# Linformer attention and an MLP mixer on one core: scores as four 64x64 matmuls, keys turned in pairs, a new order of the work

## The chip, the core and the metric

The kernel runs on one core of a Trainium2 chip. The core has a matrix engine (TensorE, called PE in the profile; its weight loads are listed apart as PEld), a vector engine (VectorE, DVE), a scalar engine (ScalarE, ACT), a general engine (GpSimd, POOL) that here issues most loads and stores, and SyncE (SP), which issues transposing transfers. Each engine works through its own list of instructions in order; semaphores make one engine wait for another. Matmuls write to PSUM, a memory of 128 partitions and 8 banks of 512 float32 columns; everything else is in SBUF, also of 128 partitions. A matmul holds a stationary operand ("weights", at most 128x128) in the array and streams a moving operand of up to 512 columns through it. If the stationary operand uses only 64 rows (partitions of its inputs) or only 64 columns (partitions of its output), the array can be used in halves or quarters.

The metric is the device time of one execution in microseconds, the median over runs.

## The reference

For each of 8 batches and 8 heads (sequence 1024, head dimension 64) the reference computes attention with keys and values projected to 64 positions, and sends the result through a mixer MLP. Cut to what matters:

```python
k_proj = einsum('ks,bhsd->bhkd', E, k)            # [8, 8, 64, 64]
v_proj = einsum('ks,bhsd->bhkd', F, v)
scores = scale * matmul(q, k_proj.transpose(0, 1, 3, 2))   # [8, 8, 1024, 64]
attn = softmax(scores)
x = matmul(attn, v_proj)      # heads side by side: [8, 1024, 512]
h = relu(x^T @ w_tok1) @ w_tok2           # 1024 -> 256 -> 1024, mixes tokens
u = x + h^T
out = u + relu(u @ w_ch1) @ w_ch2         # 512 -> 1536 -> 512, mixes channels
```

Inputs and output are float32; the kernel computes in bfloat16 with float32 sums.

## The kernel before

The work of a batch has two parts. The **front** is attention and token mixing up to u; the **back** is channel mixing, done in halves of a batch (512 rows each), sixteen in all. Both mixings use a seven-product scheme for 2x2 blocks (S_t, wT1, wT2, wS hold sums of blocks), so that the back is 84 matmuls of 256 columns "up" (L1193) and 84 "down" (L1301) per half batch, 2688 of the kernel's 3845. The front of batch b + 1 is woven into the back of batch b; batch 0's front has nothing to hide behind.

Steps of a front, with the lines that the profile shows:

- `load_heads` (the transfer is recorded at L362): keys, values and queries come in as bfloat16, two heads a transfer (256 KB in SBUF) for batch 0, four heads after that. Row `p` of the sequence block is stored with its 8 neighbours, so that a head's queries lie as [128 partitions, 8, 64].
- `kv_proj` (L529): the projections. For each of 8 steps there is one matmul with `E` (output partitions 0 to 63) and one with `F` (partitions 64 to 127), 64 stationary columns each; batches 2 to 7 use 512 moving columns, batch 1 two calls of 256, batch 0 four groups of two heads with 128. Copies (recorded at L340 on ScalarE, L338 on VectorE) take keys to `kp` or `kb`, and values to `vb`, each of them twice: `vb` of a head is a block-diagonal 128x130 operand whose 65th columns are ones.
- Keys are turned, so that the head dimension lies on partitions: for batches 0 and 1 by `k_transpose` on TensorE (L570, one 64-row matmul a head against an identity), for later ones by a transposing transfer (`k_transpose_dma`) from `kb`. The result `kT` of a head is block-diagonal too, 128x128: sequence rows of even and odd number lie on partitions 0 to 63 and 64 to 127 of `qT`, and each half meets its own copy of the keys while the other two quarters of the array hold zeros.
- Queries are turned by TensorE (`q_transpose_pe`, L618, batch 0 and 1) or by a transposing transfer.
- `scores` (L634): one matmul of 512 columns a head into one bank; ScalarE takes its exponential to `a_t` (L643).
- `attend` (L657) and, from batch 3 on, `attend_whole` (L693): per head, four matmuls of 130 columns with `a_t` as stationary operand and `vb` as moving; VectorE takes the reciprocals of the sums and multiplies into `x_sb`.
- Token mixing: by parts of 128 channels in batch 0 (`token1_part` L1073, `token2_part` L1105, `u_transpose_pe` L1134), whole in batch 1 (L724, L748), by seven products in the others (L888, L1004).

Nothing in this order is decided on the chip. Every step is a job of a `Planner`; the string `ORDER` gives the place of each job in one list for all engines (and so each engine's own list, the queues of GpSimd and SyncE among them), and `SPOTS` the PSUM bank of each use. `FILLS` names the places where a matmul on zeros (`blank`, L440) is put in front of a TensorE job. Both strings are the result of a search made beforehand with estimated durations (the second and third arguments of `pl.add`), and are read back in `plan`. Loads of batch 0 are issued first, by GpSimd: keys, values and queries by pairs of heads, then the token weights `wt1`, `wt2`, then the channel weights.

Of the kernel before, what the change touches and what calls it, by code (L numbers as in the profile page):

```python
# [15 lines left out]
    "0P0Q0R0S000T0201030U0W0X040V0s0+1G0-050u0t1I1H0x1J0y0z1L1O101209241N0v1K1P0w131M26111A1B1Q1D0625071S"  # L16
    "1T172A1g18080A1C0B1E0C1a1415191b2C1R1k2B1h1i1o1c1F1l1j1d1n1m161X1p1Y1q2D1s1U1r2E1Z1t0D1u1e1f1x1V1W1v"
    "0E272H2F0G0H1w29281+2V2I211y1-2a0F1z222b20232G2P2W2Q2M2c2J2f2X2S2g2N2K2Y2Z2d2L2R2h2e2T2O2k2i2l2U2t0I"
    "2m2p2n332u2j2x2q2r2o342-2y0J0K2v3B2s300Y2z35313C0Z2w2+320c3T3P0a3R3l3Q3F3U3D3V3J3K360d370e3W3X3Z3m38"
    "0L0N413G3p3Y3a3q3n3b3o0b3S0g0O3c420M0h3r3L3s3E3d390f3M0i3f433e3A3t3g3H0j3u3I4547465044513v48493w5x4g"  # L20
    "4h523x5y5z4k4i4A4j3y534B4J604D4l3N4o4E5-544K5+4m0o614C4F3h4p554r4L3z4n4s0p574R4q0k584u5A4S0q3-4H0l4t"
    "3j0m62634v563O654O646N666P4w594P6O5C404T6Q3+4x6e6W4Q6f6X6g3i674U6T6B6Y6Z696L5I684I3k6U6V4V6R6J6K6a6A"
    "5J6S6b6F6G5D4G6c6d0r5K5M6C4MAH6D6E6j4y4W6H5BAI6r6I0n5N6s6k6l4N4Y6u6t6m6n6h6i6o6v4Z5L5P705O6p4X6w714c"
    "726x5Q6q736z5R4a5a6y6+6-75745S5E7677787B5bAJ7C797H5T7A5c7I4d5U7D7K7E5i7J7LAK6M7NA97M7Q7FAB7G7O7R7S7P"
    "AL4b7T5V5G4z5F4+AAAOAC5W5Y5X7V5j4eAN7UAM7XAQ7W4-5f7Z7YAP7a7c7g5g7e7d7h5h7f5d7i5lAV5kAh5mAW7jAZAb5e5H"
    "Ai7bAX5n5ZAcAaAe7l7pAfAYAd5p7qAmAj817r7sAg7nAnAkAlAuAT7tAxAo5qAvAw7o7u7m82ApAr7wAy85Az5r5o7vAqAsAtA+"
    "B583B0A-5t7x86BB887y847-BC7z7k89B1B6ASB2B7BDAUARB3B880BE8J87B9BF7+8BBAB4BJ8ABM8KBGBK8LBLBHBI8M8NBP8D"
    "BNBS8OBQBO5uBR8Q8b8P8CBTBVBU8EBXBW8RBYBZ8T8y8S8cBaBb8UBc90Bd8+Be918V94Bf5v8zBgAD8WBj92Bh95Bk9E97Bi9F"
    "93Bn968FBo8-Bl9GBr9I98Bs9A9J9HAFBmBp8HBq8I99AEEn8dBuBw8X9CEp9B9L9M8jBxBvBt9WBy9OErEoEq8Z9PAG9X8g8k8h"
    "BzB+5sEj8YEk4f9DB-9aC48iC19Y8mC08lC29bC59dC79Z9c8G9e8nC68e9K8aC89f8oCB8f9g9NEs9iC99QCC8pCDEl8q8uCA9j"  # L30
    "CG9hCH8r8sC3CJE-8vEzCEF09R9oEx8wCFCLE+CNEyCO9p9kCbEv5wF1F4CK9qCP9wEmF5CQF29SF39mCMCR9xCcCIF69U9TCSCf"
    "F7CUCVCgF8Cd9y9tFBCXFCCT8t9uF9FDCYCWEw9VFGCeCtFH9vFACu9lCZCiCaFOCjDWFPCvCw9zChFECxFIDXCyFFFL9+ClCkCz"
    "FJFMDYFN9-FQ9nFRC+FSCmFKCnCoC-A1FTD0FUFVD9DaA2D1DbFWEuDAD3CpA3FXFYDeFZFaEtDfDZDcDdFd9rD4D5CqDh9sIrDB"
    "DiFeA0FbFfItFcCrA5DkFh8xInFgIsIvD2FiCsIoFjA6DoFnIuFoFkA7D7FlFmDHFrD8DpDlDgFpFvDIFsDjFqFtDmDsA4DnFwDt"
    "DJFyDEFxF+D6DFFzDqG0F-DvDGDCG8G1DrDwFuDKG2G3DyG9G5G4DLG6GBE4DMDuGCDzE5DDDxE8DNIpIqIwE9GAGDGFD+GGGEGH"
    "EBDOECE6GIDPGKD-G7J3EAGJGLEDDSJ4E7I-DQIzJ0J1EEEGGRJ2EFJ5J8GSGNDTGPGMEMJ9J6J7JDEHDUDRE0JAJBJEE1EIENGT"
    "GfEOE2GgGVJCEKA8EUGjGWEVJFGOGkJGERJHEWGQELGhESJNGmGiGUETJOGYGXJIGnI+JKDVGZGpGxJLIxGbEXEJGqJMJPHaGyJJ"
    "GaHcEYMrJSJTGcJQGzGdJRJUE3EZHeG-EbGlJVGeIyJWHbG+H0EPJXH2GoGrHdJYJZGsHfHgHiJaJbHjH3JcEQJdEcEaHhJfHsJh"
    "EdJgJiH5MsHlGtJeEfHmJjHoEgH1H6HtJkJmEhHpJlJnH4EiHkGuJoHnJrHDJsGvJpJqH7JvHqH8JtJwH9HAHBJzJxJuJ+HrMvK0"
    "HwK2HxMxK1JyHEK3K4HzJ-K5MtK6HFHuHIKCK9MyHLK7H+MwHvKDMzI0I1HMKFHyKAHCK8EeHNKGI8HGI9GwHJICHKKJIAKHKEHO"  # L40
    "IBIDKKKIKMHPKLH-HQM+KNHHIFKON7IGI2KBHSN8IEKPN3IIHTNCHRKRN4MuKVIJIHI3HUKTIKN5KWNDIQKZN9ILN1M-KaN6KXHW"
    "IRNAKYNBISIMNEKjNHHXNIKUI4NFNGI6IYHYNJKkIZNKNLNRKcKdI7NOKnIOKoKlKfIVNSNPNQNMIWKmIaKQNNKSHVKgKbI5NTIX"
    "NUKeINLeKqK-L0IbNVKhN2IcNYL3KiITNZNWKrNaL4NbIPL6NXIdNcL7IUNdKpIeIfNeKsNfIgL1KtIjKvNgNlN0NhIhNjKwL2L5"
    "L8IkLHL9LBNmKxNiNkKuKzLfNnIlLCQwNoLiLINqNpNrNsLALDIiKyQzLjLkLgLJK+LELFNtNuNvLlNwLmHZNxLwLGLMLxQ-NzNy"
    "N+O1O2LnN-LNLOL+R1LyO4LpLPO6O5O0O8LhR0O9L-LzQ+LQLoM1LSO7LqO3LRLrLTQvImOBOGOALuODOCOELvQyLsMCM2OHQxOJ"
    "M4LtOKM0LKONLLM3M5OIMDR2LUMGOLOOMHM6OPLWMEMJMFOQOSOMM7LVOFLXMKOTMIOVMLOXORLYOZLaR7MOMMRBLbMPMQMUM8R9"
    "R8MNRCOaRDLcREOWMVRARFOdOnMWOoMSMAObMcMBR4RIOrMZRJOeOcOsOpRKOuRNROOYOqR5RPMdLZOvOgOxRGOyRVRHOUMaP3Oh"
    "RWM9MeRLOfOjRSMbR6OiRTMTMfRMOkP4RaRbOlRUMRMgOmP7RQOtRXRRMhRYP5RZMjMXPiOwRcMYPmP6RdReOzMiRfPjO+PkMkMn"
    "P8RgPLR3RhMlPnPARiPlMoRjPBP9PqPoRkUzPpPDMpRlRnPCO-PMRoRpV1PFRmRqPEPrMmMqPtRrV3PNRsRtPuPsPGPHLdP0V5Ru"
    "RvPTPwRzP1V2PIV4RwPJRxRyP+P2R+PUPxPvS1PVS5R-S2PQS0S3S6U+P-PyPzQGS8SAQ0SKQ2QHQ1S9SBQIPKS4Q3QJSCPRS7SL"  # L50
    "SDQ4Q5SFQKSNPSSESHQ6QLSGQ8PWSPPXQNQ7SISOPYSRV0V6U-QASSSMQBQ9QOSTSQPOQCPaSUPPSWSXQMVBPbSVQQVCV7QRV9QY"
    "SJQDSdQPPZPcV8SZVAQZVDVEVFSbQSQTSeSfPeVIShSYSgPfQaSiQgVJVGVKQUSkQWPgQEVNScQhSrVOVPVHPdQdVLVVQeSsSlSv"
    "VWVSSwVMSaQiQfSnStSjSoVQTnVTTmVUSyVXT7VRSuSzToQjSmSxVaVYQXVZQVVcVdVeS-S+QFSpSqVbQkVfQbT0TqT8T1QlQcQn"
    "TBT2T9VgVhQmViTrTCTsVjTEQoTpVkVlQpTAVnQrVpTFTHQsTDTtVqVmTIU2QtVoTuTGT3VrVsVtTwVuTvTJU3TxVvVzVwT5TKU6"
    "TyVxVyU4T+V-TzTPV+U7T6W0U0TLT-U5W1W5U9W6UKT4TNW2UAW3ULU1W7WATQW8QqUCTRW4TMW9TOUOUDUPTUWCU8UMTVWDPhQu"
    "WBTXWEWKWFWHTWUBWGTYTaWITZUNURUETbUSUFTSUQWLWNTcWPTTUTTeWOTdUWWRTiUXWJUUWdTfWZWaWSWMUVTjWeWrWfTgWbWT"
    "WUWgWQUcWsWhWiWcUdWvWkUGTkWVUYUeWtWuWlUkX7UaUIUHUlUhWjWWUmWnUiThUJWXUjX8WwWmXBWyX9UZWoWzUnXAWYWpWqUo"
    "UbW-XCX0UpUfWxW+XEXDXFXGUgUrXHXJXqUqUsXmX1XoXKY6XnUvUtXIX2XPXrY7XuX3UuYAUwXsX5XLX4XNUxX6XpXvXQY8YBYD"
    "XwXxXtXRYEXXXUXyY9XzYGYOXYY0XVTlYHY1XWXMYPYSYQYCXaY2YTYFYRYVXZXbYWY3XcXOYUYXYIXSXeYaXfYJYKYbYgY4XTYM"
    "YYXgYZYcXdYhYeX+YLYiXiYNX-UyXhYlXjYmYdYfYoXkYxYnYjYkYsYpYqYrXlYuYvY5Z5YtYyYwZ7YzY-Y+Z0Z1Z6Z2Z8Z3Z9Z4"  # L60
    "ZA"
)
SPOTS = (
    "3142613427007634307612314207426673103142670116377263077463615421302542313140341042376756766765577757"
    "5677567656575676776765677012402414535120342241300556757665577667657656757670616706243123414252534103"
    "1030217767656565656566664736746140534132101500435323042776765656566656666572764742531530452410441031"
    "0201575666656765656667373675631354342042453105031532566576565656665666657476371031410300534153443125"
    "327676656565666566662726706421140051545432102101214756"
)
FILLS = (9, 9, 14, 14, 14, 14, 14, 14, 16, 16, 16, 16, 16, 16, 27, 27, 27, 42, 42, 72, 81, 81, 84)  # L70
# [118 lines left out]
def kernel(  # L189
# [86 lines left out]
    vb = tile_of([P, H, 2, D1], BF16, "vb")  # L276
    kT = tile_of([P, H, 2, KP], BF16, "kT")
# [3 lines left out]
    kp = wS[:KP, 0:2].rearrange("p n a b -> p (n a b)").rearrange("p (h r d) -> p h r d", h=H, r=2)  # L281
    kb = tile_of([P, H, 2, D], BF16, "kb")
# [9 lines left out]
    a_t = [tile_of([P, 2, S2], BF16, f"a{i}") for i in range(2)]  # L292
# [4 lines left out]
    rdn_t = [tile_of([P, 2, 4], F32, f"rdn{i}") for i in range(2)]  # L297
# [9 lines left out]
    nc.vector.memset(kT, 0.0)  # L307
    nc.vector.memset(kb, 0.0)
# [34 lines left out]
    def scalar():  # L343
        return None, "A"
# [162 lines left out]
    def kv_proj(b, h0, hn, due, block=False, apart=False):  # L507
# [3 lines left out]
        t = 8 * max(cols, 128) / 2400 + 0.22  # L511
        if block:
            k_to = [kb[i * KP : (i + 1) * KP, hs, i, :] for i in range(2)]
        else:
            k_to = [kp[:, hs, i, :] for i in range(2)]
        v_to = [vb[i * KP : (i + 1) * KP, hs, i, 0:D] for i in range(2)]
        of = {"k": (0, k_to, "kb" if block else "kp", ET_sb, k_sb), "v": (KP, v_to, "vb", FT_sb, v_sb)}

        def side(names):
            bk = Bank(stream[0], full=False)  # L520
# [5 lines left out]
            def mm():  # L526
                for si in range(NSI):
                    for n in names:
                        nc.tensor.matmul(  # L529
                            view(n), of[n][3][:, si, :], of[n][4][:, hs, si, :],  # L530
                            start=(si == 0), stop=(si == NSI - 1),
                        )

            pl.add(
                "PE", t, t, mm, reads=[("EFT", 0), ("EFT", 1)] + [(n, h) for n in names for h in heads],
                takes=[bk], prio=due,
                after=[("vb", i, h) for i in range(2) for h in heads] if "v" in names else (),
            ).mms = NSI * len(names)
            unit = scalar() if block else next(sides)
            for n in names:  # L540
# [1032 lines left out]
```

## Time and profile before

Three runs gave 416.75, 417.02 and 419.17 us; the median is 417.02.

| | |
|---|---|
| profiled execution: span from first to last instruction | 415.5 us (no other time of it is given) |
| TensorE clock granted | 1.000 |
| TensorE busy | 409.8 us, 3845 matmuls |
| VectorE busy | 358.8 us |
| ScalarE busy | 227.4 us |
| GpSimd busy | 66.7 us |
| matmuls of the back (L1193, L1301), busy | 198.8 and 181.8 us |
| scores (L634), 64 of them, busy | 22.8 us |
| exponentials (L643), 64 of them | 37.4 us, 600 ns each |
| first matmul on an input (L529) | at 8.57 us |
| first matmul of the back (L1193) | at 31.95 us |
| last 6 matmuls start | at 411.44 us |

A row of the timeline gives the start, the length, the engine, the line, the operation with the tiles it writes and reads, and how many equal ones in a row were merged. In the page's groups, "x64 | 22.8, 379 | 0.1" reads: 64 of them, 22.8 us busy in all, 379 ns a piece, 0.1 us of idle time of the engine in front of them. Matmuls overlap in the array: the length of one includes its way through, so the time that a stream of them costs is read from one start to the next. In brackets stands how long the engine sat idle before the row, and what released it.

### The profile page before, as it was taken

How to read it: one execution, taken by the hardware profiler on the slowest of the kernel's cores; microseconds unless marked ns; L12 is line 12 of the kernel's file. 1: busy time of each engine (PE TensorE's matmuls, PEld its weight loads, DVE VectorE, ACT ScalarE, POOL GpSimd, SP SyncE). 2: the span in 40 equal slices, each digit the busy share in tenths (PEclk: the TensorE clock that was granted, in tenths of full speed). 3: DMA queues.
4: the chain of work that ended last, by engine and by line, in shares of the span. 5: the costliest groups of instructions: out<-in, count | busy, mean ns of one | idle time of the engine just before them, and what ended most of it. 6: DMA issues, size and time to landing. Idle time of an engine off the chain costs nothing.

```text
span 415.5 us, 9448 instructions
## 1 busy us (share of the span) xinstructions
PE 409.8 (99%) x3845; PEld 349.0 (84%) x3845; DVE 358.8 (86%) x774; ACT 227.4 (55%) x434; POOL 66.7 (16%) x105
## 2 busy tenths in 40 slices
PE   8999999999999999999999999999999999999996
PEld 4589888688898889888898888988898889998885
DVE  2489898899899988989988997888999998897696
ACT  1758875376745655564465537365573656254620
POOL 8444111013010400130101220102200010000100
PEclk9999999999999999999999999999999999999999
DMA  8999999996999898679979899488982403212314
GB/s 162 204 202 205 206 206 224 168 138 101 232 167 209 137 233 134 104 170 221 217 106 189 113 184 198 83 165 135 231 152 53 100 11 144 50 53 52 153 50 154
DMA packets 96827, 62.47 MB, mean 150 GB/s; under 512 B 62096, under 2 KB 92304, under 8 KB 96784
## 3 DMA queue, kind: packets, MB, share of 16 engines
q0 software_dynamic: 35088, 45.09, 55.4%
q1 hardware_dynamic: 61056, 16.00, 22.8%
q10 hardware_dynamic: 640, 0.79, 0.5%
q8 instruction: 30, 0.49, 0.5%
q14 instruction: 13, 0.11, 0.1%
HBM read 59.24 MB, written 16.78 MB: 183 GB/s over the span
## 4 chain that ended last, share of the span: by engine, by line
PE 94%; DMA 2%; POOL 2%; DVE 1%; issue 0%; POOLq 0%; DVEq 0%
PE psum L1193 35%; PE psum L1301 35%; PE psum L1004 4%; PE psum L888 4%; PE psum L529 3%; PE psum L634 3%; DMA v_sb<-in_v_dram 2%; PE psum L693 2%; PE psum L657 1%; PE psum L1105 1%; PE psum L748 1%; PE psum L1073 1%; PE psum L724 1%; DVE x_sb L674 1%; POOL k_sb L362 1%; PE psum L618 0%
## 5 line engine op out<-in xcount | busy, mean ns | idle before, releaser
L1301 PEld LDWEIGHTS <-G 128*128 128x128 bf16 x1344 | 130.2, 98 | 17.2 <-issue 0.2
L1301 PE MATMUL psum<-wc_sb,G 128*128 128x256 bf16 x768 | 104.0, 273 | 0.0
L1193 PEld LDWEIGHTS <-wc_sb 128*128 128x128 bf16 x768 | 73.9, 98 | 10.1 <-issue 0.6
L1215 ACT ACTIVATE G<-psum 128x512 bf16<-128x512 f32 x96 | 57.3, 601 | 40.7 <-PE psum L1193 40.2
L1301 PE MATMUL psum<-wT,G 128*128 128x256 bf16 x576 | 77.8, 273 | 0.0
L1229 DVE TENSOR_TENSOR G<-G 128x512 bf16<-128x512 bf16 (+1 forms) x140 | 69.1, 514 | 0.5
L1193 PEld LDWEIGHTS <-wT 128*128 128x128 bf16 x576 | 55.6, 98 | 7.5 <-issue 0.4
L1193 PE MATMUL psum<-uT,wc_sb 128*128 128x256 bf16 x384 | 56.8, 273 | 0.0
L1193 PE MATMUL psum<-S,wT 128*128 128x256 bf16 x384 | 56.8, 273 | 0.0
L1193 PE MATMUL psum<-S,wc_sb 128*128 128x256 bf16 x384 | 56.5, 273 | 0.0
L643 ACT ACTIVATE a<-psum 128x512 bf16<-128x512 f32 x64 | 37.4, 600 | 26.3 <-PE psum L634 25.9
L1341 DVE TENSOR_TENSOR o<-psum,u 128x512 f32<-128x512 f32 x59 | 40.3, 684 | 4.7 <-PE psum L1301 3.2
L1335 POOL DMA_DIRECT2D out_dram<-o x30 | 16.3, 546 | 159.4 <-DVE o L1341 124.6
L1221 ACT COPY ub<-psum 128x512 f32<-128x512 f32 x48 | 28.1, 589 | 21.9 <-PE psum L1193 18.1
L1174 DVE CUSTOM_DVE_ANT_0 G<-psum,ub 128x512 bf16<-128x512 f32 x48 | 32.8, 683 | 6.9 <-PE psum L1193 6.5
L1236 ACT COPY psum<-psum 128x512 f32<-128x512 f32 x48 | 27.7, 577 | 19.3 <-PE psum L1193 7.7
L1174 DVE CUSTOM_DVE_ANT_0 G<-psum,ua 128x512 bf16<-128x512 f32 x48 | 32.8, 684 | 5.8 <-PE psum L1193 3.0
L1221 ACT COPY ua<-psum 128x512 f32<-128x512 f32 x48 | 28.1, 591 | 17.2 <-PE psum L1193 17.0
L362 POOL DMA_DIRECT2D v_sb<-in_v_dram x18 | 13.4, 745 | 132.7 <-DMA uT<-u 76.7
L1193 PE MATMUL psum<-uT,wT 128*128 128x256 bf16 x192 | 28.7, 273 | 0.0
L710 DVE TENSOR_TENSOR x_sb<-psum,rdn 128x512 bf16<-128x512 f32 x40 | 27.5, 688 | 0.9
L634 PE MATMUL psum<-qT,kT 128*128 128x512 bf16 x64 | 22.8, 379 | 0.1
(109 smaller groups left out, 548.2 us busy)
## 6 DMA issues: line engine op xcount, KB each, us to landing
out_dram<-o POOLq DMA_DIRECT2D x30, 512.0 KB, 4.8
k_sb<-in_k_dram POOLq DMA_DIRECT2D x14, 512.0 KB, 9.3
v_sb<-in_v_dram POOLq DMA_DIRECT2D x14, 512.0 KB, 6.5
q_sb<-in_q_dram POOLq DMA_DIRECT2D x14, 512.0 KB, 12.3
wc_sb<-in_moe_w_ch_dram POOLq DMA_DIRECT2D x6, 256.0 KB, 11.6
wc_sb<-in_moe_w_ch_dram POOLq DMA_DIRECT2D x4, 384.0 KB, 15.1
k_sb<-in_k_dram POOLq DMA_DIRECT2D x4, 256.0 KB, 7.4
q_sb<-in_q_dram POOLq DMA_DIRECT2D x4, 256.0 KB, 8.9
```

What stands on the lines that cost most here:

```text
L362: return lambda: nc.gpsimd.dma_start(out=dst, in_=src)
L634: lambda: nc.tensor.matmul(bank(bk), kT[:, h].rearrange("p c k -> p (c k)"), qT[:, h].rearrange("p j s -> p (j s)"), start=True, stop=True,),
L643: lambda: nc.scalar.activation(out=a_t[h // 2 % 2][:, h % 2], in_=bank(bk), func=ACT.Exp, scale=scale),
L710: lambda: nc.vector.tensor_tensor(out=x_sb[:, :, h * D : (h + 1) * D].rearrange("p (n c) d -> p n c d", n=2), in0=view()[:, :, :, 0:D], in ...
L1174: nc.vector._custom_dve(TENSOR_ADD_SAT, out=out, in0=in0, in1=in1, s0=FMAX, s1=0.0)
L1193: nc.tensor.matmul(t[:, c, :], w1_of(n, dd, 2 * m + c), a_of(j, n, dd), start=(n in (1, 7) and c == 0 and dd == 0), stop=(c == 1 and dd == 1),
L1215: lambda: nc.scalar.activation(out=G[:, n, cs], in_=view(src), func=ACT.Relu),
L1221: 512, lambda: nc.scalar.copy(out=dst, in_=view("y")), writes=[(name, s % 2)],
L1229: 512 * len(both), lambda: f(out=G[:, n, c], in0=G[:, a, c], in1=G[:, b, c]), ps=False,
L1236: 512, lambda: nc.scalar.copy(out=view("y"), in_=view("x")), takes=[bk["y"]],
L1301: nc.tensor.matmul(to, G[:, G_OF[n], cc, t * P : (t + 1) * P], w2_of(n, cc), start=(n in opens and (t == 0 or alone) and cc == 0), stop=(c ...
L1341: 512, lambda: nc.vector.tensor_add(out=dst, in0=view(src), in1=u_of(sh, dh)),
```

## The change

- **Scores.** `scores` now takes pairs of heads. Per pair `g` there are two banks, one for each half (even and odd sequence rows). Four matmuls with 64 rows and 64 columns of the array each: half `half` of the partitions (`rows`) holds the turned keys of head `2g + i` and its queries; the output goes to partitions `64 i` and up of bank `(g, half)`. The order within a pair alternates the quarters. A call does one pair in batch 0 and two pairs (four banks) in the other batches, so there are two calls a batch instead of eight.
- **Layouts that follow.** `a_t` holds a pair of heads on its partitions, with the halves side by side (four tiles instead of two). `vb` is block-diagonal over the two heads of a pair (half as large), `kT` holds 64 columns a head, the same on both partition halves, without zeros. `attend` works on a pair and a half of the sequence; the number of its matmuls (32 of 130 columns a batch), reciprocals and multiplies is as before. Values are copied once instead of twice; keys are copied to both places of `kb`, now for all batches (`kp` is gone). `kT` and `kb` are no longer cleared at the start.
- **Keys of batches 0 and 1.** `k_transpose` turns a pair of heads with one full 128x128 matmul against the identity, and its result is taken out with one copy instead of two. The transposing transfer of the later batches has half the size.
- **Order.** `ORDER`, `SPOTS` and `FILLS` are new throughout. There are 21 filler matmuls instead of 23. Loads of batch 0 are issued in the order v0, k2, q0, k0, q2, v2, k6, q6, k4, v4, q4, wt1, wt1, v6, wt2 (the number is the first of the two heads); before it was k0, q0, v0, k2, v2, q2, k6, k4, v4, q4, q6, v6, wt1, wt1, wt2. Job estimates change slightly (the projection's 0.22 us of extra time is now 0.03, and jobs carry a `mode`).

```diff
-FILLS = (9, 9, 14, 14, 14, 14, 14, 14, 16, 16, 16, 16, 16, 16, 27, 27, 27, 42, 42, 72, 81, 81, 84)
+FILLS = (20, 20, 20, 20, 20, 20, 20, 20, 20, 20, 20, 20, 20, 20, 20, 20, 33, 33, 49, 67, 92)
...
-    vb = tile_of([P, H, 2, D1], BF16, "vb")
-    kT = tile_of([P, H, 2, KP], BF16, "kT")
+    vb = tile_of([P, HP, 2, D1], BF16, "vb")
+    kT = tile_of([P, H, KP], BF16, "kT")
...
-    kb = tile_of([P, H, 2, D], BF16, "kb")
+    kb = tile_of([P, HP, 2, D], BF16, "kb")
...
-    nc.vector.memset(kT, 0.0)
-    nc.vector.memset(kb, 0.0)
...
             for n in names:
-                for i in ((0, 1) if n == "k" else (1, 0)):
-                    copy(
-                        unit, cols, of[n][1][i], lambda n=n: view(n),
-                        writes=[(of[n][2], i, h) for h in heads], uses=[bk],
-                    )
+                for i in range(2):
+                    rows = slice(i * KP, (i + 1) * KP)
+                    if n == "v":
+                        copy(
+                            unit, cols // 2, vb[rows, pairs, i, 0:D], lambda i=i: odd("v", i),
+                            writes=[("vb", h) for h in heads if h % 2 == i], uses=[bk],
+                        )
+                    else:
+                        copy(
+                            unit, cols, kb[rows, pairs],
+                            lambda i=i: odd("k", i)[:, :, None, :].to_broadcast([KP, hn // 2, 2, D]),
+                            writes=[("kb", h) for h in heads if h % 2 == i], uses=[bk],
+                        )
...
         def mm():
-            for h in range(hn):
+            for h in range(0, hn, 2):
                 nc.tensor.matmul(
-                    view()[:, h, :], kp[:, h0 + h].rearrange("k r d -> k (r d)"),
-                    ident[:KP, :KP], start=True, stop=True,
+                    view()[:, h : h + 2, :].rearrange("p h k -> p (h k)"),
+                    kb[:, (h0 + h) // 2].rearrange("k r d -> k (r d)"), ident, start=True, stop=True,
                 )
...
-    def scores(h, due):
-        bk = Bank(stream[0], full=False)
-        pe(
-            1, 512,
-            lambda: nc.tensor.matmul(
-                bank(bk), kT[:, h].rearrange("p c k -> p (c k)"),
-                qT[:, h].rearrange("p j s -> p (j s)"), start=True, stop=True,
-            ),
...
+    def scores(pairs, due):
+        bks = {(g, half): Bank(stream[0]) for g in pairs for half in range(2)}
+        def mm():
+            for g in pairs:
+                for half, i in ((0, 0), (1, 1), (0, 1), (1, 0)):
+                    rows, to = (slice(n * D, (n + 1) * D) for n in (half, i))
+                    nc.tensor.matmul(
+                        bank(bks[g, half])[to], kT[rows, 2 * g + i],
+                        qT[rows, 2 * g + i].rearrange("p j s -> p (j s)"), start=True, stop=True,
+                    )
...
+        for (g, half), bk in bks.items():
+            act(
+                512,
+                lambda g=g, half=half, bk=bk: nc.scalar.activation(
+                    out=a_t[g][:, half], in_=bank(bk), func=ACT.Exp, scale=scale
+                ),
+                writes=[("a", g, half)], uses=[bk],
+            )
...
+    def attend(g, half, due, span):
+        def unit(jn, due):
...
+            def mm():
+                for k, jj in enumerate(jn):
+                    for c in range(2):
+                        at = (2 * half + jj) * P
+                        nc.tensor.matmul(
+                            view()[:, k, c].rearrange("p i d -> p (i d)"), a_t[g][:, c, at : at + P],
+                            vb[:, g].rearrange("k i d -> k (i d)"), start=True, stop=True,
+                        )
...
+        if span == 2:
+            unit((0, 1), due)
+        else:
+            unit((0,), due)
+            unit((1,), due)
...
-        unit(0.4, lambda t: scores(0, t))
-        unit(0.4, lambda t: scores(1, t))
-        for h in range(H):
-            if h + 2 < H:
-                unit(0.4, lambda t, h=h: scores(h + 2, t))
-            if b >= WHOLE:
-                unit(0.5, lambda t, h=h: attend_whole(h, t))
-                continue
+        unit(1.0, lambda t: scores((0, 1), t))
+        for g in range(HP):
+            if g == 1:
+                unit(1.0, lambda t: scores((2, 3), t))
             for half in range(2):
-                unit(0.25, lambda t, h=h, half=half: attend(h, half, t))
+                unit(0.5, lambda t, g=g, half=half: attend(g, half, t, 2 if b >= WHOLE else 1))
```

More of the change, by code (lines that the diff above doesn't have):

```diff
@@ L21 @@
[L21 to L30, printed above, removed]
@@ L510, in kv_proj @@
         cols = hn * D
[L511 to L517, printed above, removed]
+        t = 8 * max(cols, 128) / 2400 + 0.03
+        pairs = slice(h0 // 2, (h0 + hn) // 2)
+        of = {"k": (0, ET_sb, k_sb), "v": (KP, FT_sb, v_sb)}
         def side(names):
-            bk = Bank(stream[0], full=False)
+            bk = Bank(stream[0], full=hn == H)
             def view(n):
@@ new lines, in scores @@
+    def scores(pairs, due):
[8 more added lines that the diff above has]
+                    )
+        heads = [2 * g + i for g in pairs for i in range(2)]
+        j = pl.add(
+            "PE", len(pairs) * MM[512], len(pairs) * MM[512], mm,
+            reads=[(n, h) for n in ("kT", "qT") for h in heads], takes=list(bks.values()), prio=due,
+            after=[("a", g, half) for g in pairs for half in range(2)],
+        )
+        j.mms, j.mode = 4 * len(pairs), 3
+        for (g, half), bk in bks.items():
[5 more added lines that the diff above has]
+                writes=[("a", g, half)], uses=[bk],
+            )
@@ L844, in one @@
             )
[L846 to L847 removed]
+        one(5, wS[:, 0], a21, a22, add=True)
         one(7, wS[:, 2], a11, a21)
[L850 removed]
+        one(6, wS[:, 1], wS[:, 0], a11, deps=(5,))
         one(3, a21, a12, wS[:, 1], deps=(6, 7, 5), after=wt1_all)
@@ L1424 @@
         q_transpose_pe(hp, due + 1.5)
-        for h in (2 * hp, 2 * hp + 1):
-            scores(h, due + 2)
-        for h in (2 * hp, 2 * hp + 1):
-            for half in range(2):
-                attend(h, half, due + 3)
+        scores((hp,), due + 2)
+        for half in range(2):
+            attend(hp, half, due + 3, 1)
     for p0, pn in PARTS:
```

233 lines of the change are left out of this document (96 added, 137 removed).

## The prediction

> **What bounds the kernel now.** I read the page from the top: busy shares, the slices, the chain, then the group of the scores.
>
> ```profile
> span 415.5 us, 9448 instructions
> ...
> PE 409.8 (99%) x3845; PEld 349.0 (84%) x3845; DVE 358.8 (86%) x774; ACT 227.4 (55%) x434; POOL 66.7 (16%) x105
> ...
> PE   8999999999999999999999999999999999999996
> ...
> PE 94%; DMA 2%; POOL 2%; DVE 1%; issue 0%; POOLq 0%; DVEq 0%
> ...
> L634 PE MATMUL psum<-qT,kT 128*128 128x512 bf16 x64 | 22.8, 379 | 0.1
> ```
>
> TensorE (PE) is the bound in every slice but the first and last. The 379 ns of one score is a pipelined length and not what it costs. The cost is the step from one start to the next, which the timeline of PE gives:
>
> ```profile
> 92.55 0.38 PE L634 MATMUL psum<-qT,kT 128*128 128x512 bf16 x1
> 92.76 0.60 PE L1193 MATMUL psum<-S,wc_sb 128*128 128x256 bf16 x4
> ```
>
> A score costs 0.216 us (0.21 in these rounded rows, 0.216 over all its steps); likewise a 256-column matmul costs 0.109, a 130-column one 0.057. From 24.03 to its last matmul near 412.1 PE never waits: of its gaps beyond those steps all but two of 0.1 us lie at changes of the tile shape. A projection shows such a change:
>
> ```profile
> 149.97 0.82 PE L1301 MATMUL psum<-wT,G 128*128 128x256 bf16 x6
> 150.71 0.40 PE L529 MATMUL psum<-k_sb,EFT_sb 128*64 128x512 bf16 x1
> 150.72 0.40 PE L529 MATMUL psum<-v_sb,EFT_sb 128*64 128x512 bf16 x1
> 150.95 0.38 PE L529 MATMUL psum<-k_sb,EFT_sb 128*64 128x512 bf16 x1
> 150.96 0.38 PE L529 MATMUL psum<-v_sb,EFT_sb 128*64 128x512 bf16 x1
> ...
> 152.25 0.38 PE L529 MATMUL psum<-k_sb,EFT_sb 128*64 128x512 bf16 x1
> 152.25 0.38 PE L529 MATMUL psum<-v_sb,EFT_sb 128*64 128x512 bf16 x1
> 152.56 0.61 PE L888 MATMUL psum<-u,wS 128*128 128x256 bf16 x4
> ```
>
> Two things are to be seen. Keys and values, in two halves of the array's columns, start within 0.01 us and step together by 0.215: two matmuls for the price of one. And a visit to another shape costs extra: the last L1301 starts at 149.97 + 5 x 0.109 = 150.52, the next start comes 0.09 late, the second pair 0.02 late, the first L888 0.31 after the last pair instead of 0.215, the one after it 0.01 late. Together **0.22 us a visit**, 0.11 a change.
>
> The first 24 us are bound by loads, which land one after another; the GpSimd timeline shows the pace:
>
> ```profile
> 12.72 0.56 POOL L362 DMA_DIRECT2D wt_sb<-in_moe_w_tok_dram  x1 [0.56 <-DMA v_sb<-in_v_dram]
> 13.99 0.54 POOL L362 DMA_DIRECT2D wt_sb<-in_moe_w_tok_dram  x1 [0.72 <-DMA q_sb<-in_q_dram]
> ```
>
> One load of 256 KB in 1.27 us. Values that are third, fifth and ninth in line start their projections at 9.22, 12.47 and 17.59: place p lands at 12.4 + 1.27 (p - 5).
>
> **The change, part by part (after 24 us).**
> - Scores, batches 1 to 7: 56 matmuls x 0.216 = 12.10 become 28 groups of four 64x64 matmuls. If the four run at once, a group costs one step, 28 x 0.216 = 6.05: **-6.05**. The rows show the two column halves at once, but never two row halves. So a group lies between 0.216 (all at once) and 0.432 (row halves in turn); below 0.216 is excluded, since 512 columns pass. I take 0.216: nearest is the projection's row, and each row half here has its own bank and its own input rows.
> - Changes of shape: 10 visits (8 projections, 2 turnings of keys in batch 1) become 22 (8 projections, 14 scoring calls), one scoring call standing directly before a projection and sharing a change. 22 x 0.22 - 0.11 - 10 x 0.22 = **+2.53**. Entry to a four-tile shape is not in the trace; I take the projection's price, bounds 0 and 0.4 a visit.
> - Keys of batch 1 turned pair by pair: 8 x 0.04 = 0.3 become 4 x 0.056 = 0.22: **-0.08**.
> - Attention times values stays at 32 matmuls of 130 a batch, with as many reciprocals and multiplies: 0. The exponentials stay 64 x 0.600. ScalarE's copies of values halve in width (0.590 to about 0.372, the row of 256), two clears on VectorE and half of the keys' transposing DMA go: 0, for PE waits for none of these after 24 us.
> - Four banks are now taken at once, and each first attend needs two exponentials: about 0.2 after the group, 2 x 0.60, 0.1 to start, so 1.5 us. The new order leaves 1.5 to 2.0 us of PE work there in batches 1, 2, 3, 4 and 7 and over 3.9 in 5 and 6. ScalarE's order is fixed by the plan too; one more copy of 0.6 in between shows as a PE wait. I take **+0.2**, bounds 0 and 7 x 0.6 = 4.
>
> Sum after 24 us: -6.05 + 2.53 - 0.08 + 0.2 = -3.4.
>
> **The start.** Batch 0 also needs less PE work: scores 0.86 less, two filler matmuls 0.43, two changes 0.22, key turns 0.08, 1.6 in all. It buys nothing: PE waits for loads there. What counts is when PE stops waiting and what is left then. The new queue order is values 0, keys 2, queries 0, keys 0 (4th, 11.2 us), and so on; queries 4 are 11th (20.1), the last values 14th (23.9 where they landed at 21.4), second token weights unchanged (26.4). After queries 4: transposes 0.45, ScalarE copies of 0.2 each and the 1.01 one to about 22.0, scores, then three exponentials to 23.9, attends and a token matmul group to 24.8, where the last values' projection stands. Before had 388.1 us from 24.03 on. At 24.8 the new order has 24 token matmuls less ahead (1.34) and one projection more (0.67): 388.1 - 3.6 - 0.67 = 383.8, plus the 0.2 above and 0.3 for the last pair's reciprocals and multiplies (4 x 0.17 + 4 x 0.416 = 2.3 us of VectorE, covered by about 2 us of PE work). PE ends at 24.8 + 384.3 = 409.1, against 412.1: **-3.0**. Bounds on the start: 0.8 better (no wait for the exponentials) to 1.5 worse (one load slot late).
>
> The end keeps its 3.4 us of last adds and stores. Span 412.5. The profiled execution's time is given by its span alone; the median of the runs, 417.02, lies 1.5 above it, and I add that: **414.0 us**, 0.7% less.
>
> **The Trainium skill** on the four tiles: its page TensorE: Matmul & The Clock Gate (Part 3, What overlaps and what doesn't) has weight loads overlap running matmuls only where the row group differs. By that the second column half of each row half would load only after the first had run, and each group would be two rounds with bare loads. The trace disagrees for the two column halves: pairs on the same 128 rows step at 0.215. No run here shows two row halves.
>
> **Rivals.**
> 1. Row halves take turns. For: no row shows two row halves running together. Against: the column halves do. A group then costs 0.432, so nothing is saved but 2.53 of changes is paid: 414.0 + 6.05 + about 0.4 in batch 0 = **420.5**, slower than before. It decides from about 0.32 a group, where 28 x 0.108 eats the gain of 3.0.
> 2. Two rounds with bare weight loads, 2 x (0.216 + 0.110, the length of a 64-column load): 28 x 0.436 = 12.2 more, **426**. Against: the step of 0.215 above. The rule just cited says this.
> 3. The new order waits where the old did not: exponentials late by a copy in most batches, or a key, query or value load late (the whole order is new, and nothing in it gives way on the chip). For: the 1.5 to 2.0 us above are tight. Against: old waits after 24 us are 0.2 in all. Price 2 to 4: **416 to 418**.
> 4. The start does better: PE's savings there count because the last values no longer gate. 1.5 less: **412.5** or below.
>
> **How the numbers follow.** Forecast 0.60 (412 to 415.5), rival 1 0.09, 2 0.03, 3 0.13, 4 0.15. 1% is 4.2 us, about what a measurement of this kernel can tell: faster means below 412.85. Rival 4 and a quarter of the forecast's spread lie there: 0.30. Rival 2 and half of rival 1 lie above 421.2: 0.08. The rest, 0.62, is within 1%. The range leaves out rivals 1 and 2 and the tails of 3 and 4: 411.5 to 418.5.
>
> **What would show it.** Four L636 matmuls starting within some 0.02 us and the next four 0.216 later (right), or two starting 0.2 after the other two (rival 1). The last matmul before a scoring call and the first after it show the visit's 0.22. PE idle, released by ScalarE's exponentials, would be rival 3; the last values' projection at 24 or at 25 decides the start. I am wrong above all if a group's step is not one matmul's, or if the first 27 us lose more than a load slot.

## The result

The changed kernel took **418.75 us** (median of 19, 416.86 to 423.01) where the kernel before took 417.18 (19, 416.59 to 419.17) beside it: a ratio of 1.0049 (here and below of the means), interval [1.0029, 1.0069]. Forecast were 414.0, in a range that ended at 418.5. Two later measurements of the same two kernels, on two different chips, gave 0.9997 [0.9981, 1.0013] and 1.0002 [0.9984, 1.0019]. So the change brought nothing in any of the three, and in one it cost half a per cent. Both facts have to be explained.

The page of the changed kernel, in the order used for before: span, engines, TensorE by slices, the chain.

```profile
span 418.4 us, 9560 instructions
...
PE 407.5 (97%) x3899; PEld 344.6 (82%) x3899; DVE 357.4 (85%) x771; ACT 221.3 (53%) x429; POOL 66.8 (16%) x105
...
PE   8799999989999999999999999999999999999995
...
PE 83%; DVE 7%; DMA 5%; POOL 2%; issue 1%; ACT 0%; SPq 0%; POOLq 0%; DVEq 0%
```

TensorE was at 9 in every slice of before but the ends; now the ninth slice (83.7 to 94.1 us) has an 8, and its share of the chain is 83% in place of 94%. (The second slice, 10.5 to 20.9 us, has a 7: batch 0 has less work for TensorE now, and waits for loads and copies there.) Its group of scores has 128 rows of 64x64 and names the wait:

```profile
L636 PE MATMUL psum<-qT,kT 64*64 64x512 bf16 x128 | 10.4, 389 | 2.6 <-DMA kT<-kb 1.8 <-ACT kT L335 0.6 <-ACT qT L335 0.2
```

The timeline of TensorE (start, length, line, times in a row) shows an ordinary scoring call, and then the one that waited:

```profile
63.91 0.38 PE L1287 MATMUL psum<-wc_sb,G 128*128 128x256 bf16 x2
64.22 0.63 PE L636 MATMUL psum<-qT,kT 64*64 64x512 bf16 x8
64.78 0.61 PE L1179 MATMUL psum<-S,wc_sb 128*128 128x256 bf16 x4
...
90.80 0.60 PE L1179 MATMUL psum<-S,wc_sb 128*128 128x256 bf16 x4
93.21 0.63 PE L636 MATMUL psum<-qT,kT 64*64 64x512 bf16 x8 [1.82 <-DMA kT<-kb]
93.77 0.61 PE L1179 MATMUL psum<-uT,wT 128*128 128x256 bf16 x4
94.22 0.77 PE L1179 MATMUL psum<-uT,wc_sb 128*128 128x256 bf16 x4
94.78 1.06 PE L1179 MATMUL psum<-S,wT 128*128 128x256 bf16 x4
95.64 1.06 PE L1179 MATMUL psum<-S,wc_sb 128*128 128x256 bf16 x4
```

Eight scores and both changes of shape lie between 64.02 (the last L1287 start, 63.91 + 0.109) and 64.78: 0.760 us, of which 0.109 belong to the L1287. The first group of four and the second stand 0.240 us apart in the unrounded rows. At 91 us the same call begins 1.89 us late because the turned keys of batch 2 have not landed. A little later four matmuls take 0.86 us (94.78 to 95.64) in place of 0.44. The windows (of their columns: the stretch, its length, PE busy, and after POOL the granted clock, DMA share and GB/s) say why:

```profile
91.00:95.00 4.00, 2.18 (x22) 1.25 (x20) 2.03 (x4) 1.92 (x4) 0.00 (x0) 0.94 1.39 130
95.00:100.00 5.00, 5.00 (x38) 3.95 (x36) 3.36 (x11) 3.51 (x7) 0.74 (x1) 0.71 0.61 138
```

The granted clock is at half for 3.41 us, from 94.51. Before had 1.00 in both of these stretches. TensorE's gaps beyond a normal step in that stretch add up to 1.64 us.

What the late keys have beside them shows in the lists of SyncE and GpSimd. Before, the keys of batch 2 were turned ahead of the first half of u (the second goes out at 91.26):

```profile
78.59 1.23 SPq L553 DMA_TRANSPOSE kT<-kb  x1
80.69 13.63 SPq L796 DMA_TRANSPOSE uT<-u  x2
```

Now they come behind it, and so does a load of values that the landing of this half of u releases:

```profile
79.36 2.82 SPq L783 DMA_TRANSPOSE uT<-u  x1
82.41 1.73 SPq L599 DMA_TRANSPOSE qT<-q_sb  x1
84.24 1.83 SPq L557 DMA_TRANSPOSE kT<-kb  x1
...
84.32 0.74 POOL L357 DMA_DIRECT2D v_sb<-in_v_dram  x1 [9.73 <-DMA uT<-u]
```

The end is the third difference. The last rows of TensorE and of ScalarE's queue, after:

```profile
409.31 0.60 PE L1179 MATMUL psum<-S,wc_sb 128*128 128x256 bf16 x4
409.74 1.47 PE L1287 MATMUL psum<-wT,G 128*128 128x256 bf16 x12
411.05 2.79 PE L1287 MATMUL psum<-wc_sb,G 128*128 128x256 bf16 x24
...
413.68 1.65 ACTq L1321 DMA_DIRECT2D out_dram<-o  x3
```

and the same queue before:

```profile
411.06 1.43 ACTq L1335 DMA_DIRECT2D out_dram<-o  x3
```

Before, the first of these three stores was issued 0.93 us ahead of the last matmul's start (411.99). Now it is issued 0.11 behind it (413.57). The one of 256 KB among them went out 0.93 ahead before and 0.51 behind now. From the last matmul's start to the end of the span it is 3.46 us before and 4.80 after: to the last issue 0.76 and 1.41, from there to its landing 1.77 and 2.45.

### The profile page after: what moved, and what is told of

Same layout as the page of the kernel before. It is cut to its first block, busy times and chain, and to the rows that moved or that the text cites. A ratio compares the mean times of both kernels' runs of the same rounds, so it can differ in the third digit from the quotient of the medians.

```text
span 418.4 us, 9560 instructions
## 1 busy us (share of the span) xinstructions
PE 407.5 (97%) x3899; PEld 344.6 (82%) x3899; DVE 357.4 (85%) x771; ACT 221.3 (53%) x429; POOL 66.8 (16%) x105
## 4 chain that ended last, share of the span: by engine, by line
PE 83%; DVE 7%; DMA 5%; POOL 2%; issue 1%; ACT 0%; SPq 0%; POOLq 0%; DVEq 0%
PE psum L1179 32%; PE psum L1287 31%; PE psum L990 4%; PE psum L874 4%; PE psum L671 3%; PE psum L520 3%; DMA q_sb<-in_q_dram 3%; DMA kT<-kb 2%; PE psum L636 2%; DVE x_sb L691 1%; DVE G L1215 1%; PE psum L1091 1%; PE psum L711 1%; POOL k_sb L357 1%; PE psum L735 1%
## 5 line engine op out<-in xcount | busy, mean ns | idle before, releaser
L1287 PEld LDWEIGHTS <-G 128*128 128x128 bf16 x1344 | 129.8, 98 | 17.3 <-issue 1.4
L1287 PE MATMUL psum<-wc_sb,G 128*128 128x256 bf16 x768 | 100.5, 273 | 0.0
L1201 ACT ACTIVATE G<-psum 128x512 bf16<-128x512 f32 x96 | 56.1, 601 | 42.3 <-PE psum L1179 41.7
L1287 PE MATMUL psum<-wT,G 128*128 128x256 bf16 x576 | 75.7, 273 | 0.0
L691 DVE TENSOR_TENSOR x_sb<-psum,rdn 128x256 bf16<-128x256 f32 (+1 forms) x88 | 46.3, 540 | 1.9
L651 ACT ACTIVATE a<-psum 128x512 bf16<-128x512 f32 x64 | 34.6, 603 | 10.1 <-PE psum L636 10.1
L671 PE MATMUL psum<-vb,a 128*128 128x130 bf16 x256 | 25.0, 222 | 0.3 <-DVE vb L333 0.2
```

The costliest lines, as they stand in the source:

```text
L651: lambda g=g, half=half, bk=bk: nc.scalar.activation(out=a_t[g][:, half], in_=bank(bk), func=ACT.Exp, scale=scale),
L671: nc.tensor.matmul(view()[:, k, c].rearrange("p i d -> p (i d)"), a_t[g][:, c, at : at + P], vb[:, g].rearrange("k i d -> k (i d)"), start ...
L691: lambda: nc.vector.tensor_tensor(out=x_sb[:, rows, g * P : (g + 1) * P].rearrange("p (n c) (i d) -> p n c i d", c=2, i=2), in0=view()[:, ...
L1201: lambda: nc.scalar.activation(out=G[:, n, cs], in_=view(src), func=ACT.Relu),
L1287: nc.tensor.matmul(to, G[:, G_OF[n], cc, t * P : (t + 1) * P], w2_of(n, cc), start=(n in opens and (t == 0 or alone) and cc == 0), stop=(c ...
```

## The experiments

All times are medians; ratios are against the kernel before, measured beside each run. In the first four runs before had 417.47.

**The load behind the second half of u.** In before, the load of values for batch 3 (512 KB) went out at 85.50 us, when the keys had long landed (81.61); in the new order it goes out 0.08 us after the keys' transfer. This run puts it behind the second transposing transfer of `u` (`late` holds the load's job and that transfer's; the lines left out turn round which of the two has to come first).

```diff
+        moved, behind = self.late
+        order.remove(moved)
+        order.insert(order.index(behind) + 1, moved)
...
```

> One load of values (batch 3, heads 0 to 3) is issued behind the second transposing transfer of u of batch 1, instead of behind the first; the rest is the changed kernel. Theory A (this load collides with the transposing transfer of the keys of batch 2, so the scores of batch 2 come 2 us late and TensorE's clock then drops for 3.4 us): the keys land within 4.5 us of their issue instead of 8.9, the wait of 2.0 us at 91 us and the 2.6 us lost at half clock are gone, 415 to 416 us. Rival B (the transposing transfer is slow by itself at this place): it takes 8 to 9 us again, the wait stays, 418.5. Rival C (another wait takes its place, on the queries or on u): 417 to 418.

416.71 us, 0.9978 [0.9969, 0.9987]. The transfers being issued between 84.0 and 85.5 us (names, queue, operation, us to landing), after and here:

```profile
v_sb<-in_v_dram POOLq DMA_DIRECT2D x1, 512.0 KB, 8.6
qT<-q_sb SPq DMA_TRANSPOSE x1, 4.3
kT<-kb SPq DMA_TRANSPOSE x1, 8.9
```

```profile
qT<-q_sb SPq DMA_TRANSPOSE x1, 4.8
kT<-kb SPq DMA_TRANSPOSE x1, 2.5
```

The keys take 2.5 us without the load beside them and 8.9 with it, and the scores no longer wait:

```profile
90.67 0.60 PE L1182 MATMUL psum<-S,wc_sb 128*128 128x256 bf16 x4
91.19 0.63 PE L639 MATMUL psum<-qT,kT 64*64 64x512 bf16 x8
91.75 0.61 PE L1182 MATMUL psum<-uT,wT 128*128 128x256 bf16 x4
```

There is no half-clock stretch ahead of the last matmul, and this one starts at 410.12 in place of 413.57. So the collision is shown to cause the wait. The unedited changed kernel was not run beside this one; where it was run beside others (below), it took 417.63, and three kernels with the load moved 416.34 to 417.06.

**Fillers in the wait.** Nine matmuls on zeros ahead of batch 2's first scores, the load left where it was.

```diff
...
+            if j is pl.covered:
+                for _ in range(9):
+                    nc.tensor.matmul(
+                        banks[j.takes[0].at], zero, zero[:, None, :].to_broadcast([P, NJ, P]), start=True, stop=True
+                    )
```

> The changed kernel with nine matmuls on zeros (9 x 0.216 = 1.9 us) in front of the first scores of batch 2, so that TensorE is busy while it would wait there. Theory A (the clock drops because TensorE stood idle for 2 us): no stretch at half clock, granted clock 1.000, the place costs 2.0 us instead of 4.6, 416.5 to 418. Rival (the clock drops for another reason): half clock stays for 3.4 us after 94 us, 418.5 to 420.5.

419.14 us, 1.0034 [1.0021, 1.0047]. In its profiled execution the keys landed after 5.6 us, ahead of the scores, so there was no wait for the fillers to cover and they only cost their own time. As a test of the clock it was inconclusive. It showed that the landing varies while the load stays beside the keys.

**The first store on SyncE.** The 256 KB store of the last half batch on the other queue.

```diff
-            queue = (nc.sync if sh else nc.scalar) if last else nc.gpsimd
+            queue = (nc.sync if sh or (halves == (0,) and t is None) else nc.scalar) if last else nc.gpsimd
```

> The changed kernel with one of the last three stores on SyncE's queue instead of ScalarE's. Theory (the last store waits for its queue: it is issued 0.7 us after its data are ready): the last issue follows its data by under 0.1 us, the time from the last matmul to the end falls from 4.8 to 3.8 to 4.2 us, 0.6 to 1.0 us less than the changed kernel. Rival (the end is set by the transfers, not by the issue): no change.

416.73 us, 0.9989 [0.9976, 1.0002]. The end did not get shorter: 4.91 us. The last store was issued 0.12 us after the last operation of VectorE ended, where the changed kernel has 0.68, so the delay at the queue was gone as expected; but it landed 3.1 us later in place of 2.45. The gain at the queue was lost in the transfer. That the three stores in flight share the transfers is the likely reason, not shown. Again there was no wait at 91 us (keys landed after 6.3 us).

**Both edits.** The diffs of the first and third run together.

> The load behind the second transposing transfer of u and the store on the other queue, together. If both theories hold the sum is 407.7 to the last matmul without waits, plus about 1 us of small waits, 4.0 at the end, 1.7 around the span: 414 to 415 us, 0.5 to 0.8% below the kernel before. If the wait of 2 us only moves: 416.5 or more.

416.72 us, 0.9989 [0.9979, 0.9999]: no better than the load alone, end 4.66 us.

**The changed kernel again** was run beside three others (before there 417.60), with nothing edited, because two runs that left the load in place had shown no wait.

> The changed kernel with nothing altered, beside the others on this chip. What is open: in its first profile the keys' transposing transfer of batch 2 landed 8.9 us after its issue and the scores waited 1.98 us, while two kernels that keep this part unaltered (the fills, the store's queue) had it land in 5.6 and 6.3 us with no wait. Collision theory: the transfer's landing varies from execution to execution with the values' load beside it, so the profile shows a landing anywhere from 5.5 to 9 us after the issue; where it is above 6.8 us the scores wait, and where the wait reaches about 2 us the granted clock halves for 3.4 us. Median between 417.0 (no wait) and 419 (wait and half clock), with a wide spread. Rival: the first executions were on a slower chip and the wait is fixed: the wait of 1.8 to 2.0 us again, 418.7.

417.63 us, 0.9997, all ten executions within 416.30 to 418.09. The wait is there, shorter, by the view of waits (line, what for, total, times, longest):

```profile
PE psum L636 <- DMA kT<-kb: 1.1, 1, 1.1
```

The scores were 1.22 us late, the keys took 8.4 us, and the clock stayed at 1.00 after the wait. So not every wait halves the clock.

**A new order of the last 30 jobs**, on top of the moved load: the last up product ahead of the seventh down block, the second down block ahead of the fourth.

```diff
...
+        end = [2122, 2123, 2183, 2169, 2176, 2177, 2147, 2170, 2180, 2129, 2165, 2178, 2181, 2182, 2193, 2184, 2179, 2195, 2196, 2185, 2187, 2186, 2188, 2189, 2190, 2194, 2191, 2192, 2197, 2198]
+        order = [j for j in order if self.jobs.index(j) not in end] + [self.jobs[i] for i in end]
```

> The values' load behind the second half of u, as before, and the last 30 jobs in another order: the last up product (of batch 7) ahead of the seventh down block, and the second down block ahead of the fourth, so that out's first 256 KB leave while TensorE still works. Theory (the end is 4.7 us and not 3.4 because three of the stores leave together after the last matmul): the end goes from 4.67 to about 3.5 us, with the last matmul where it was (410.1): 1.2 us less than with the load alone, 415.5, the fastest of all. Rival (TensorE will wait elsewhere instead, for VectorE, which has five more operations to do in the last 4 us): the last matmul comes 0.5 to 1 us later and the time stays at 416.5.

416.34 us, 0.9969 [0.9957, 0.9981], the lowest median of all, though the interval overlaps that of the load alone, and 0.3% under the unedited changed kernel measured beside it. Half of the theory fell: the end is 4.18 us, not 3.5. The last issue is 0.76 after the last matmul's start, as in before, but its store lands 2.49 later where before needed 1.77: the two stores ahead of it went out 0.2 to 0.3 later than in before and landed 0.4 to 0.8 later. The rival did not occur. The last matmul starts at 410.58, 0.45 later than with the load alone, but it is 0.48 later already at the first projection after 24 us and 0.45 at 150 and at 400 us: this execution was behind from the start, and TensorE lost nothing to the new end.

**Keys late, without a load beside them.** On top of the moved load, the keys' transfer behind that of the second half of the queries.

```diff
+        keys, turned = self.jobs[650], self.jobs[644]
+        order.remove(keys)
+        order.insert(order.index(turned) + 1, keys)
```

> The values' load behind the second half of u, as before, and the transposing transfer of batch 2's keys behind that of the second half of its queries on SyncE, so that the keys land late without a load beside them. Clock theory: the scores wait about 2 us for the keys, the granted clock then halves for about 3.4 us and costs another 2 to 2.6, so the time is that of the load alone plus 4 to 4.6: about 421. Rival (the half clock in the first profile had another cause, and a wait costs only itself): plus 2, about 418.7, and no half-clock stretch behind the wait.

417.06 us, 0.9990 [0.9977, 1.0002]. The keys landed at 91.71 and the scores were only 0.15 us late, so this dose was too small to test the clock.

**Keys later still**, behind the second transfer of `u` (the same lines with job 478 in place of 644; before there 417.54).

> As the late keys (values' load behind the second half of u), but the transposing transfer of batch 2's keys also behind that of the second half of u on SyncE: issued about 89 to 92 us after the start, landing at 94 to 96, with the scores due at 91.4. The scores wait 3 to 4 us, with no load beside the transfer. Clock theory (a wait of about 2 us or more halves the granted clock for 3.4 us): a half-clock stretch behind the wait in the profile, and the time is that of the load alone (416.7) plus 3 to 4 plus 2 to 2.6: 421.7 to 423.3. Rival (the wait costs only itself): 419.7 to 420.7 and a granted clock of 0.997 or more.

420.90 us, 1.0073 [1.0048, 1.0097]. The keys take 2.5 us, with no load beside them until one is issued at 93.75, but go out only at 91.83 and land at 94.30. Timeline, then windows:

```profile
90.86 0.60 PE L1185 MATMUL psum<-S,wc_sb 128*128 128x256 bf16 x4
94.35 0.83 PE L642 MATMUL psum<-qT,kT 64*64 64x512 bf16 x8 [2.89 <-DMA kT<-kb]
```

```profile
91.00:95.00 4.00, 1.11 (x12) 0.31 (x10) 1.45 (x3) 1.09 (x3) 1.13 (x2) 0.95 0.65 129
95.00:100.00 5.00, 5.00 (x39) 3.88 (x36) 2.63 (x7) 3.27 (x7) 4.35 (x7) 0.69 1.06 144
```

The half clock is back, again for 3.41 us (from 94.64), without the collision that made the keys late in the changed kernel. The last matmul starts at 414.82, 4.70 later than with the load alone: 2.96 for the wait, 1.62 for the clock, 0.19 by which this execution was behind from 24 us on, less 0.07 of other gaps. The total of 420.9 lies between the two expectations because I had priced the wait at 3 to 4 and the clock at 2 to 2.6. All five executions show a mean clock of 0.995 or 0.996; with the load alone none of ten was below 0.997, and of before, beside this run, four of 18. So the wait is the cause of the half clock here; the price is half of 3.41, less the gaps that would have been there.

**Row halves one after the other in the list.** On the moved load and the store on SyncE.

```diff
-            for g in pairs:
-                for half, i in ((0, 0), (1, 1), (0, 1), (1, 0)):
+            for half in range(2):
+                for g, i in ((g, i) for g in pairs for i in range(2)):
...
```

> The values' load behind the second half of u and out's first store on SyncE, and in the scores first row half 0 of both pairs, then row half 1, so that the two row halves are not interleaved: in a call of 32 matmuls, each row half's 16 go two at a time (column halves) at one step each. If four tiles together need the two row halves side by side, a call takes 16 steps of 0.109 (1.74 us) in place of 8 (0.87): 14 calls by 0.87 = 12 us more, about 428.9. If only the neighbours in the list count, the row halves overlap nowhere but where they meet, which gives the same but for one step. Rival: the row half does not matter and a column half already frees the array (two tiles at a time were never the bound): no change, 416.7.

416.92 us, 0.9974 [0.9960, 0.9988]. The call costs 0.768 us in place of 0.760:

```profile
91.35 0.63 PE L639 MATMUL psum<-qT,kT 64*64 64x512 bf16 x8
91.92 0.28 PE L1182 MATMUL psum<-uT,wT 128*128 128x256 bf16 x1
```

My price of 12 us counted 16 steps in place of 8 a call; a call has 8 matmuls, so two at a time would be 4 steps of 0.216 in place of 2, 6 us in all. If each matmul started in the order of the list, the fifth and sixth would run beside the third and fourth, 3 steps, 3 us in all. None of these came. Four matmuls still start within 17 ns and the next four 0.24 us later, although the third and fourth of the list need the same quarters as the first two. The rows do not name the quarter, so this is a deduction: two streams of 512 columns cannot share a quarter in 0.24 us, so the third and fourth to start must be the fifth and sixth of the list, overtaking.

**Each score made twice**, on the moved load, to price a group and see whether it sets the time.

```diff
-                for half, i in ((0, 0), (1, 1), (0, 1), (1, 0)):
+                for half, i in ((0, 0), (1, 1), (0, 1), (1, 0)) * 2:
```

> The values' load behind the second half of u, and each score matmul made twice in a row of its call (the second writes the same values again), so a call has four groups of four in place of two. If a group of four matmuls of 512 columns costs TensorE one step (0.216 us, 0.23 with its weights) and TensorE sets the time: 28 groups after 24 us by 0.216 to 0.23 = 6.0 to 6.4 us, and up to 0.9 more from the four groups ahead of 24 us: 722 is not reached, 422.7 to 424.0. If the four are not at once but two and two: twice that, 429. If TensorE's time does not set the end: 416.7.

(The "722" in that text is a slip and stands for nothing.) 423.17 us, 1.0127 [1.0102, 1.0152], 6.5 us above the load alone, inside the 422.7 to 424.0 of the first theory.

```profile
92.55 0.60 PE L1182 MATMUL psum<-S,wc_sb 128*128 128x256 bf16 x4
93.07 1.06 PE L639 MATMUL psum<-qT,kT 64*64 64x512 bf16 x16
94.06 0.61 PE L1182 MATMUL psum<-uT,wT 128*128 128x256 bf16 x4
```

The four groups of a call start 0.240, 0.216 and 0.216 apart; a call costs 1.192 in place of 0.760, 0.432 more for two groups, 6.05 over 14 calls. The four run at once and their time is on the path.

**The changed kernel a third time**, for the spread.

> The changed kernel once more, for the spread. In its first 19 executions the seven with a mean granted clock of 0.996 or less took 420.1 to 423.0 us and the twelve others 416.9 to 419.2; in the ten of the second time none was below 0.997 and the longest was 418.1. If the half-clock stretch comes from the long wait for the keys, executions with 0.996 or less are again the slowest, by 2 us and more; the median is 417.5 to 418.8.

418.20 us (416.38 to 419.06, 12), 1.0002. The wait:

```profile
93.05 0.63 PE L636 MATMUL psum<-qT,kT 64*64 64x512 bf16 x8 [1.57 <-DMA kT<-kb]
93.61 0.61 PE L1179 MATMUL psum<-uT,wT 128*128 128x256 bf16 x4
94.06 0.60 PE L1179 MATMUL psum<-uT,wc_sb 128*128 128x256 bf16 x4
```

Full speed after it (0.44 for four matmuls). No execution had a mean clock below 0.997, so the expected group of slowest ones at 0.996 did not appear here. What the profiles say of the keys together:

| profiled execution | load beside | issue to landing, us | scores late by, us | half clock ahead of the last matmul |
|---|---|---|---|---|
| changed kernel, first | yes | 8.9 | 1.89 | 3.41 us |
| changed kernel, third | yes | 8.7 | 1.64 | none |
| changed kernel, second | yes | 8.4 | 1.22 | none |
| store on SyncE | yes | 6.3 | 0 | none |
| fillers | yes | 5.6 | 0 | none |
| load behind | no | 2.5 | 0 | none |
| both edits; new order; row halves; scores twice | no | 2.7; 3.1; 2.6; 4.0 | 0 | none |
| keys late | no | 4.2 | 0.15 | none |
| keys later | in its last 0.6 us | 2.5 | 2.96 | 3.41 us |

In the first measurement seven of 19 executions had a mean clock of 0.996 or less (0.992 in the slowest two) and took 420.1 to 423.0; the other twelve took 416.9 to 419.2. One stretch of 3.41 us is 0.004 of the mean. In the second and third measurements there were none in 22 executions. That is about half of the difference between 1.0049 and 1.000: the mean of the twelve others is still 1.0024 of before. A longer wait for the keys may be the rest; only one of these executions was profiled. Two things stay open. Why the keys landed later in the first measurement was not found. And the mean does not say where a stretch lies: in the three later measurements nine of 75 executions of before also had 0.995 or 0.996 (four of 18 in the last, 418.3 to 419.6), and which part of those was slow was not profiled. Means of 0.998 and 0.999 need no stretch of this kind: in the profiled executions that have them the clock is at half from 2.5 to 4.5 us behind the last matmul's start on, where no matmul is left to slow.

## Why the prediction was wrong

Against the profiled execution (span 418.37, last matmul's start 413.57), step by step:

- **The start: right.** The last values' projection (L520) starts at 24.79; 24.8 was forecast. (In the other profiled executions with single scores it is 24.64 to 25.12.)
- **Scores in fours: right.** A second group costs 0.216 (doubled calls) and 0.240 as first pair of groups. Rival 1 and rival 2 did not occur. The rule of the Trainium skill that the prediction cites, by which weights load beside running matmuls only in another row group, is contradicted: the doubled call steps at 0.216 with four loads of weights per step, two in each row half.
- **Changes of shape: right.** A call of 0.760 less 0.109 and two steps of 0.216 leaves 0.219; 0.22 was taken. The call takes 0.757 to 0.761 in all 13 that did not wait.
- **Rest of TensorE's work:** without any wait the last matmul would start at 413.57 - 1.89 - 1.64 - 2.39 = 407.65, where the sum without its 0.5 of waits gave 408.6. Of these 0.95, 0.78 are small gaps of before, which the 388.1 carried along, and 0.11 is the step of the last matmul, which 408.6 includes. So this term was right within 0.1.
- **The small waits: a term of the wrong size.** I took 0.2 for late exponentials and 0.3 for the last pair. Gaps of more than 3 ns beyond a normal step between full-array matmuls, apart from those of the keys and of the clock, add up to 2.39 us after 24 us, against 0.78 in before (which the prediction read as 0.2): 0.22 at 26.7, 0.33 at 133.3, 0.18 at 123.9, 0.15 at 111.9, and many of 0.12 or less. With the 0.78 that the 388.1 held, the sum had 1.28 for them. My bounds of 0 and 4 held them; my value did not. The variant with the load moved has 2.6, so no run here is known to take them away.
- **Rival 3 was the case, and it had 0.13.** Its words "a key, query or value load late" are what happened. The step that failed is the argument against it, "old waits after 24 us are 0.2 in all": the old order's small waits say nothing of the new order's transfers. The queues of GpSimd and SyncE were said to be part of the order, but I followed them only for batch 0's loads; for the later batches I never set the issue of a transfer beside what is in flight with it. The order of before had the keys issued at 78.59 and landed at 81.61, with no such load. The rival's price of 2 to 4 also left out that a wait may bring a second cost. Here it was 1.89 + 1.64 = 3.53.
- **"The end keeps its 3.4 us": failed.** It is 4.80, 1.4 more (1.34 against the 3.46 of before, counted from the same point). The order of the last products is as new as the rest, and the stores follow it. With the load moved, where nothing waits at 91 us, it is 4.67.
- **The time around the span:** 1.77 in this execution (420.14), where 1.5 was added.

The sum: 412.5 - 0.06 (work) + 1.11 (small waits, 2.39 in place of 1.28) + 3.53 (late keys and clock) + 1.29 (the end, from the end of the last matmul's step, 4.69 in place of 3.4) = 418.37. So of the 3.0 us of TensorE's work that I expected to see at the end, the work itself went. Over 2 us came back as small waits and a longer end even where the keys are in time (416.7 with the load moved: 0.2% under before instead of 0.7%), and the late keys took the rest and more.

## What to carry to other kernels

When a fixed order is replaced, price the new waits from the new order: for each transfer that TensorE will need, set its issue beside the large loads in flight then, and give it the landing time of a shared transfer (here 5.6 to 8.9 us), not that of a lone one (2.5). Read the last few matmuls of the new order too, since it is they, not the old tail, that say which stores leave last. And a gap in TensorE's work that nears 2 us should be priced with a possible stretch of half clock behind it (here 1.6 us of TensorE's time).

## What the runs showed of the hardware

- The keys' transposing transfer of batch 2, 2.5 to 4.2 us with no load beside it, takes 5.6 to 8.9 beside one load of 512 KB, varying from one execution to the next.
- The granted clock halves for 3.41 us after a wait that made the scores 1.89 or 2.96 us late, not after 1.22 or 1.64. In both cases the stretch begins 3.4 us after the last matmul ahead of the wait (91.12 to 94.51, 91.19 to 94.64), but this is no fixed delay: at the end of the kernel it begins 2.5 us (row halves) to 4.5 us (store on SyncE) after the last matmul's start. The Trainium skill, TensorE: Matmul & The Clock Gate, Part 1 (What's actually happening), has a free-running window of 3413 ns, after an idle one of which the clock goes to half; the length of the stretch agrees. Its section "Why this matters for your kernels" asks for no gaps over some 3 us; here the measurement decides otherwise, since a gap under 2 us was enough. Whether a gap of 1.64 us would do where it falls otherwise in such a window is not shown.
- Four 64x64 matmuls of 512 columns, one in each quarter of the array, run in the time of one (0.216 us), and their order in the list hardly matters (0.768 against 0.760 us a call).
